# Preparing a second factor in steps of two pieces, with a third staging buffer, and a last sum taken straight from PSUM

## The chip, the cores and the metric

The kernel runs on one core of a Trainium2 chip. The time is device microseconds (us) from start to end of one execution; the kernel before takes 779.91 us, the median of three runs (779.88 to 781.03). A profile is one execution taken by the hardware profiler; its span is 776.9 us. Five engines work side by side: TensorE (PE in the profile; PEld is its weight load), VectorE (DVE), ScalarE (ACT), GpSimd (POOL) and SyncE (SP), whose queue issues most of the transfers. [...]

## What is computed

The first half is an attention without softmax, for 8 batches, 8 heads, 576 tokens and a head size of 64; the second is a feed-forward block with a product of two projections in its middle.

```python
kv = np.einsum('bhsd,bhse->bhde', k, v)
out = np.einsum('bhsd,bhde->bhse', q, kv)
rms = np.sqrt(np.mean(out * out, axis=-1, keepdims=True) + 1e-06)
x = (out / rms * g_norm)          # heads side by side: 4608 tokens x 512
a = x @ w1                        # 512 x 1024
b = x @ w2                        # 512 x 1024
h = a * b @ w3                    # 1024 x 1024
return h @ w_out                  # 1024 x 512
```

All of it is in fp32. Nothing stands between the last two products, so the kernel multiplies `w3 @ w_out` once (1024 x 512, kept in `w3o_sb`) and projects `a * b` with that.

## The kernel before

**Groups.** The tokens are worked in nine groups of 512 (512 of each batch's 576, and one group, number 8, of the 64 that are left of every batch). They run in the order 0 to 6, 8, 7. Each group has two stages. The *gates* (`gates`, called for p = 0 to 3) compute `a * b`: matrix products at L617, ScalarE copies out of PSUM (L630, L752), VectorE sums and products (L753 to L757). The *projection* multiplies `a * b` with the second factor `w3o`. In group 0 that is `project`; from group 1 on it is `project_twice`.

**Fewer products by sums.** Both stages use Winograd's form of Strassen's scheme: a 2 x 2 block product with seven block products instead of eight, paid for by sums of blocks on VectorE. `project_twice` applies it twice: seven outer products, each split again into seven inner ones. For that, each of the seven blocks of the second factor (b11, t1, t2, b22, b12, b21, t4, as `b_blocks` lists them) needs its own four inner combinations t1, t2, t3, t4. They are the same for all groups, so they are computed once.

**Preparing the second factor.** `prepare_b` is a generator that does this while group 1's gates run. Its piece n (0 to 6) takes block n, y: four VectorE subtractions (L810 to L813) put t1, t2 and t4 in a staging buffer of 128 x 768 values and t3 in place over b12 of y; then two transfers on the sync queue store y (L814) and the stage (L817) as part n of the DRAM tensor `w3o_l2`. The stage is `o_sbs[n % 2]`, so piece n may write it only when piece n - 2's store has read it. `o_sbs` holds a group's output too; group 0's output is stored from there (L776). The last block, t4, is also stored as it is, before piece 6 changes it (L799, part 7): the last group multiplies its last product in one level only and needs it unchanged. L812 of piece 6, which writes over a part of it, waits for that store.

**Who calls it.** The loop over groups hands `gates` a function `between`, called twice in each of the four gates of a group, so eight times. Each call first runs one step of the next batch's attention (`steps`): loads of k, v and q (L95, L105, L110), the products of k and v (L326) and with q (L409), the normalisation (L377 to L387, which writes `xn`) and the transposes of q and of `xn`. A transpose goes by way of GpSimd, which splits the words into halves (L284, L286), a DMA transpose on the sync queue (L288), and GpSimd again, which puts them together (L298). `xn` has one buffer and serves as the target of its own transposes, so the next normalisation's last instruction (L387) waits for the L298 of the one before. In group 1, `between` then draws up to three pieces:

```python
for _ in range(2):
    next(preparing, None)
if len(loaded_b) == 0 and next(preparing, 0) == 0:
    for _ in range(3):
        load_b()
```

That makes 3, 3 and 1 pieces in the first three calls; the third also issues the first three `load_b` (L831). These bring parts 0, 1 and 2 back from DRAM into `streams`, three buffers laid over the places of `w3o_sb` and of the blocks t2 and t4. Later parts are loaded one at a time within `project_twice`.

**The order of the work.** TensorE, GpSimd and SyncE run in the order in which the code is written. For VectorE and ScalarE the framework's planner sets the order, but from the last gate of a group to the end of its projection VectorE too follows the code.

**The last group's end.** In `project_twice`, `keep` copies a product's seven blocks from PSUM to SBUF on ScalarE (L900, L901), `add` sums PSUM onto a kept one on VectorE (L928, L929), and `finish` turns seven blocks into four of output by four VectorE sums (L910 to L913) and stores them. The tile `u` that takes u2, u3 and u4 has one buffer. The fifth product is kept as `u3`; its sum with the kept `p5` (L975) is finished as block (1, 1), and u3 itself as block (1, 0). In the last group `last_block` finishes u3, multiplies the last product in one level (L941), adds it (L947) and stores it in two halves (L922).

Of the kernel before, what the change touches and what calls it, by code (L numbers as in the profile page):

```python
# [21 lines left out]
def kernel(  # L22
# [32 lines left out]
    nc = tc.nc  # L55
    PSUM = bass.MemoryType.PSUM
    P = 128
# [9 lines left out]
    N = G // 2  # L67
# [14 lines left out]
    def bank(pool, tag):  # L82
        return pool.tile([P, 512], FP32, name=tag, tag=tag)
# [523 lines left out]
    def late_tile(name):  # L607
        return late_pool.tile([P, 7, P], FP32, name=name[0] if name[0] == "u" else name)

    def winograd(lhsT, rhs, chunks, done, between=lambda: None):  # L610
# [27 lines left out]
        product("s2", "t2", r1)  # L638
        u2 = keep("u2", r1)
        between()  # L640
        product("s4", "b22", r2)
        done("c12", r2, u2)
# [40 lines left out]
    o_sbs, ab_sums, w3o_sums, streams, inner_sums = [], [], [], [], []  # L683
# [103 lines left out]
    def b_blocks():  # L787
        b = {
            (i, j): w3o_sb[:, i * NF:(i + 1) * NF, j * N:(j + 1) * N]
            for i in range(2) for j in range(2)  # L790
        }
        t1, t2, t4 = w3o_sums
        return [b[0, 0], t1, t2, b[1, 1], b[0, 1], b[1, 0], t4]

    def prepare_b():

        for n, y in enumerate(b_blocks()):
            if n == 6:
                nc.sync.dma_start(  # L799
                    out=w3o_l2[7, :, 0:1024].rearrange("p (f n) -> p f n", n=N), in_=y  # L800
                )
            b11, b12, b21, b22 = (
                y[:, 2 * i:2 * i + 2, j * P:(j + 1) * P] for i in range(2) for j in range(2)
            )

            stage = o_sbs[n % 2].rearrange("p m n -> p (m n)")[:, 0:6 * P]
            t1, t2, t4 = (t.rearrange("p (c n) -> p c n", n=P) for t in (
                stage[:, i * 2 * P:(i + 1) * 2 * P] for i in range(3)
            ))
            nc.vector.tensor_sub(t1, b12, b11)  # L810
            nc.vector.tensor_sub(t2, b22, t1)
            nc.vector.tensor_sub(b12, b22, b12)  # L812
            nc.vector.tensor_sub(t4, b21, t2)  # L813
            nc.sync.dma_start(  # L814
                out=w3o_l2[n, :, 0:1024].rearrange("p (f n) -> p f n", n=N), in_=y
            )
            nc.sync.dma_start(out=w3o_l2[n, :, 1024:PART], in_=stage)  # L817
            yield

    loaded_b = []  # L820
# [33 lines left out]
    def project_twice(T, last, ahead):  # L854
        def store(half):
            if T < B:
                rows = out[T * S:T * S + G, :].rearrange("(p j) f -> p j f", j=J)
                nc.sync.dma_start(out=rows[:, 2 * half:2 * half + 2, :], in_=o_sbs[half])
                return
            for m in range(2):  # L860
                for l in range(2):
                    b = 2 * (2 * half + m) + l
                    nc.sync.dma_start(
                        out=out[b * S + G:(b + 1) * S, :], in_=o_sbs[half][l * L:(l + 1) * L, m, :]
                    )

        def products(n, ps=None):

            new = ps is None or n == 5
            if ps is None:  # L870
                ps = [bank(ps_mm, "mm").rearrange("p (i n) -> p i n", n=P) for _ in range(2)]
            a11, a12, a22, s1, s2, s4, s3 = inner[n]
            w = loaded_b[7 * done[T] + n]
            b = w[:, 0:1024].rearrange("p (f n) -> p f n", n=N)
            b11, t3, b21, b22 = (
                b[:, 2 * i:2 * i + 2, j * P:(j + 1) * P] for i in range(2) for j in range(2)
            )
            t1, t2, t4 = (
                w[:, 1024 + 256 * i:1280 + 256 * i].rearrange("p (c n) -> p c n", n=P)
                for i in range(3)  # L880
            )
            seen = set()
            for place, x, y in (
                (0, a11, b11), (3, a12, b21), (1, a22, t4), (2, s1, t1), (6, s2, t2), (5, s4, b22),
                (4, s3, t3),
            ):
                to, i = ps[place // 4], place % 4
                for c in range(2):
                    nc.tensor.matmul(  # L889
                        to[:, i, :], lhsT=x[:, c, :], rhs=y[:, c, :],  # L890
                        start=new and place // 4 not in seen,
                        stop=(c == 1),
                        skip_group_check=True,
                    )
                    seen.add(place // 4)
            return ps

        def keep(name, ps):
            t = late_tile(name)
            nc.scalar.copy(t[:, 0:4], ps[0])  # L900
            nc.scalar.copy(t[:, 4:7], ps[1][:, 0:3])  # L901
            return t

        def finish(z, half, j):

            def wide(i):
                return z[:, i:i + 1].to_broadcast([P, 2, P])

            dst = o_sbs[half][:, :, j * N:(j + 1) * N].rearrange("p m (i n) -> p m i n", n=P)
            nc.vector.tensor_add(z[:, 6], z[:, 6], z[:, 0])  # L910
            nc.vector.tensor_add(z[:, 4:6], z[:, 4:6], wide(6))
            nc.vector.tensor_add(dst[:, 1], z[:, 1:3], wide(4))
            nc.vector.tensor_add(dst[:, 0], z[:, 3:6:2], z[:, 0:3:2])  # L913
            if not last:
                if j == 0:
                    store(half)
            elif (half, j) != (1, 0):
                store_block(half, j)

        def store_block(half, j, a=0, b=2, queue=nc.sync):  # L920
            rows = out[T * S:T * S + G, j * N:(j + 1) * N].rearrange("(p j) f -> p j f", j=J)
            queue.dma_start(  # L922
                out=rows[:, 2 * half + a:2 * half + b, :],
                in_=o_sbs[half][:, a:b, j * N:(j + 1) * N],
            )

        def add(z, ps):
            nc.vector.tensor_add(z[:, 0:4], ps[0], z[:, 0:4])  # L928
            nc.vector.tensor_add(z[:, 4:7], ps[1][:, 0:3], z[:, 4:7])  # L929

        done[T] = len(done)

        def last_block(z):

            a22, t4 = ab[1][:, :, 1], loaded_b[7 * done[T] + 6]
            t4 = t4.rearrange("p (f n) -> p f n", n=N)
            finish(z, 1, 0)
            ps = bank(ps_mm, "mm").rearrange("p (m n) -> p m n", m=2)
            for m in range(2):
                for p in range(NF):  # L940
                    nc.tensor.matmul(  # L941
                        ps[:, m, :], lhsT=a22[:, p, m * P:(m + 1) * P], rhs=t4[:, p, :],
                        start=(m == 0 and p == 0), stop=(p == NF - 1), skip_group_check=True,
                    )
            for m in range(2):
                dst = o_sbs[1][:, m, 0:N]
                nc.vector.tensor_add(dst, dst, ps[:, m, :])  # L947
                store_block(1, 0, m, m + 1, nc.scalar if m else nc.sync)


        r1 = products(0)
        p1 = keep("p1", r1)
        load_b()
        sum_inner(2)
        for f in ahead:
            f()
        r2 = products(1)
        p5 = keep("p5", r2)
        load_b()
        sum_inner(3)  # L960
        products(2, r1)
        z = keep("u2", r1)
        load_b()
        sum_inner(4)
        products(3, r2)
        load_b()
        add(z, r2)
        sum_inner(5)
        finish(z, 0, 1)
        products(4, r1)  # L970
        z = keep("u3", r1)
        load_b()
        if not last:
            sum_inner(6)
        nc.vector.tensor_add(p5, p5, z)  # L975
        finish(p5, 1, 1)
        products(5, r2)
        load_b()
        add(p1, r2)
        finish(p1, 0, 0)  # L980
        if last:
            last_block(z)
        else:
            products(6, r1)
            load_b()
            finish(keep("u4", r1), 1, 0)
# [3 lines left out]
    w3o_l2 = dram.tile([8, P, PART], FP32, name="w3o_l2")  # L990
# [9 lines left out]
    with tc.manual_schedule(  # L1000
# [6 lines left out]
        for e in range(2):  # L1007
            nc.scalar.dma_start(
                out=g_row[:, e * D:(e + 1) * D], in_=g_norm.rearrange("(o d) -> o d", o=1)
# [76 lines left out]
    for n, T in enumerate(groups):  # L1086
        pieces = steps(T + 1) if n + 2 < NG else iter([])

        def between():
            next(pieces, lambda: None)()  # L1090
            if T == 1:
                for _ in range(2):
                    next(preparing, None)
                if len(loaded_b) == 0 and next(preparing, 0) == 0:
                    for _ in range(3):
                        load_b()

        for p in range(NF):
# [28 lines left out]
        last = n + 1 == NG  # L1127
# [6 lines left out]
        preparing = prepare_b()  # L1134
# [32 lines left out]
```

## Time and profile before

| what | value |
|---|---|
| time, median of 3 | 779.91 us |
| span of the profile | 776.9 us |
| TensorE busy | 761.9 us (98%) |
| VectorE busy | 542.0 us (70%) |
| ScalarE busy | 249.5 us (32%) |
| GpSimd busy | 135.1 us (17%) |
| bytes moved by DMA | 132.55 MB |
| group 1, gates (167.84 to 228.49 us) | 60.65 us |
| group 1, projection (228.49 to 251.96 us) | 23.47 us |
| group 3, gates (328.20 to 381.78 us) | 53.58 us |
| group 3, projection (381.78 to 403.66 us) | 21.88 us |

The profile is read by its stretches. The chain of waits, followed back from the last instruction, names for each moment the instruction that the end depended on. The timeline lists each engine's instructions with start, length, engine, line, operation, output and inputs, and in brackets how long the engine had been idle just before and what ended that. The busy times by stretch compare stages of different groups. In the names, `raw` is the memory of the conversion tiles, in which the blocks, the sums and `o_sbs` lie later on; `w3o_l` is the DRAM tensor of the prepared factor.

### The profile page before, as it was taken

The page shows a single profiled execution, that of the slowest core. Times are in us where ns is not written, and L with a number is a line of the kernel's source. Part 1 is how long each engine was busy: PE and PEld are TensorE (multiplying, and loading weights), DVE is VectorE, ACT ScalarE, POOL GpSimd, SP SyncE. Part 2 cuts the span into 40 slices and gives each one's busy share as a digit, 9 for nine tenths or more (in the row PEclk, how much of TensorE's full clock was granted, in tenths as well). Part 3 has the DMA queues.
Part 4 walks back from the last instruction along what each step waited for, and adds up shares of the span by engine and source line. Part 5 has one row for each costly group of instructions (what it writes and reads, how often), then busy time and mean ns, then how long its engine had stood idle before and what let it go on. Part 6 is the DMA issues. An engine that isn't in the chain of part 4 may idle for free.

```text
span 776.9 us, 14423 instructions
## 1 busy us (share of the span) xinstructions
PE 761.9 (98%) x5775; PEld 660.9 (85%) x5775; DVE 542.0 (70%) x1086; ACT 249.5 (32%) x483; POOL 135.1 (17%) x132
## 2 busy tenths in 40 slices
PE   8999999999979999999999999999999999999997
PEld 6455788888869889988998899889988998898896
DVE  6978999439579567945784778567756864594566
ACT  6687643212212332232222322332133222122120
POOL 0000000221330253033204520331144000000000
PEclk9999999999999999999999999999999999999999
DMA  9996650238998844884388448734852470074014
GB/s 316 339 331 182 200 149 30 82 102 260 243 290 281 223 99 109 282 231 110 90 281 220 109 117 271 220 95 133 271 108 51 138 249 0 1 244 143 1 57 167
DMA packets 132775, 132.55 MB, mean 171 GB/s; under 512 B 76644, under 2 KB 120676, under 8 KB 132708
## 3 DMA queue, kind: packets, MB, share of 16 engines
q1 hardware_dynamic: 130256, 116.81, 51.1%
q10 hardware_dynamic: 2452, 14.81, 5.5%
q8 instruction: 46, 0.75, 0.4%
q14 instruction: 21, 0.17, 0.1%
HBM read 100.27 MB, written 16.38 MB: 150 GB/s over the span
## 4 chain that ended last, share of the span: by engine, by line
PE 89%; DVE 5%; DMA 3%; SPq 1%; ACT 1%; issue 1%; POOL 0%; DVEq 0%; ACTq 0%; POOLq 0%
PE mm L617 55%; PE mm L889 21%; PE mm L596 7%; PE at L326 2%; PE at L409 2%; DMA raw<-in_moe_w_out_dram 1%; PE at L583 1%; SPq L288 1%; DVE c L756 1%; DMA w3o_l<-raw 1%; DMA xn<-xT 1%; PE at L345 1%; DVE ab L757 0%; DMA raw<-in_moe_w_dram 0%; DMA out_dram<-raw 0%
## 5 line engine op out<-in xcount | busy, mean ns | idle before, releaser
L617 PE MATMUL mm<-xT,w_sb 128*128 128x256 f32 x768 | 176.2, 379 | 0.0
L617 PEld LDWEIGHTS mm<-xT,w_sb 128*128 128x128 f32 x768 | 145.5, 190 | 20.0 <-issue 0.5
L617 PE MATMUL mm<-xc,ws 128*128 128x256 f32 x576 | 132.2, 382 | 4.9 <-ACT p L630 4.9
L617 PEld LDWEIGHTS mm<-xc,ws 128*128 128x128 f32 x576 | 110.2, 192 | 20.8 <-ACT p L630 5.7
L756 DVE TENSOR_TENSOR c<-mm,u 128x512 f32<-128x512 f32 x36 | 24.9, 691 | 105.8 <-PE mm L617 105.8
L630 ACT COPY u<-mm 128x512 f32<-128x512 f32 x74 | 43.4, 587 | 141.6 <-PE mm L617 133.3
L630 ACT COPY p<-mm 128x512 f32<-128x512 f32 x74 | 43.3, 587 | 87.9 <-PE mm L617 78.5
L617 PE MATMUL mm<-xc,w_sb 128*128 128x256 f32 x288 | 69.3, 383 | 0.0
L889 PE MATMUL mm<-w3o_sb,raw 128*128 128x128 f32 x500 | 62.3, 275 | 0.6 <-DVE raw L849 0.6
L596 PE MATMUL mm<-chunks,ab 128*128 128x512 f32 x128 | 60.2, 601 | 1.7 <-DVE chunks L165 1.6
L617 PE MATMUL mm<-xT,ws 128*128 128x256 f32 x256 | 61.3, 382 | 0.0
L284 POOL COPY xT<-xn 128x1024 uint16<-128x1024 uint16 x26 | 32.3, 1271 | 162.2 <-DVE xn L387 162.1
L617 PEld LDWEIGHTS mm<-xc,w_sb 128*128 128x128 f32 x288 | 53.6, 190 | 7.8 <-ACT u L630 0.3
L757 DVE TENSOR_TENSOR ab<-c 128x256 f32<-128x256 f32 x108 | 58.0, 537 | 3.0
L889 PEld LDWEIGHTS mm<-w3o_sb,raw 128*128 128x128 f32 x500 | 59.0, 192 | 0.9 <-DVE raw L849 0.8
L617 PEld LDWEIGHTS mm<-xT,ws 128*128 128x128 f32 x256 | 48.3, 191 | 6.8
L378 DVE TENSOR_REDUCE inv<-sq 128x8 f32<-128x512 f32 (+1 forms) x40 | 23.4, 626 | 36.0 <-ACT sq L377 36.0
L756 DVE TENSOR_TENSOR c<-p,u 128x512 f32<-128x512 f32 x36 | 25.6, 711 | 27.6 <-ACT u L630 27.4
L889 PE MATMUL mm<-w3o_sb,ab 128*128 128x128 f32 x336 | 43.8, 275 | 0.3 <-DVE ab L851 0.3
L889 PEld LDWEIGHTS mm<-w3o_sb,ab 128*128 128x128 f32 x336 | 41.0, 192 | 0.8 <-DVE ab L851 0.5
L596 PEld LDWEIGHTS mm<-chunks,ab 128*128 128x128 f32 x128 | 21.9, 190 | 22.7 <-issue 15.8
L900 ACT COPY u<-mm 128x512 f32<-128x512 f32 x23 | 13.5, 587 | 85.4 <-DVE raw L913 64.7
(157 smaller groups left out, 1138.7 us busy)
## 6 DMA issues: line engine op xcount, KB each, us to landing
w3o_sb<-w3o_l SPq DMA_DIRECT2D x26, 896.0 KB, 5.0
raw<-in_moe_w_dram SPq DMA_DIRECT2D x31, 512.0 KB, 7.3
raw<-w3o_l SPq DMA_DIRECT2D x13, 896.0 KB, 5.1
w3o_sb<-w3o_l ACTq DMA_DIRECT2D x11, 896.0 KB, 4.7
k_sb<-in_k_dram SPq DMA_DIRECT2D x32, 256.0 KB, 3.7
v_sb<-in_v_dram SPq DMA_DIRECT2D x32, 256.0 KB, 4.3
q_sb<-in_q_dram SPq DMA_DIRECT2D x32, 256.0 KB, 4.2
out_dram<-raw SPq DMA_DIRECT2D x14, 512.0 KB, 3.5
```

The source lines that it names most:

```text
L284: nc.gpsimd.tensor_copy(to, src.rearrange("p a n w -> p w a n"))
L288: nc.sync.dma_start_transpose(out=turned.bitcast(U16).rearrange("p (a t) -> p a t", t=P), in_=apart.bitcast(U16))
L326: nc.tensor.matmul(kv_ps[e * D:(e + 1) * D, r - rs[0], :], lhsT=k_sb[:, e, cols] if j < J else kl[:, 2 * r + e, :], rhs=v_sb[:, e, cols] i ...
L378: nc.vector.tensor_reduce(out=inv[:, i], in_=sq.rearrange("p (h d) -> p h d", d=D), axis=AX.X, op=ALU.add)
L409: nc.tensor.matmul(o_ps[l][tokens, n * D:(n + 1) * D], lhsT=qT[r][rows, e, i, tokens], rhs=kv_b[rows, e, r, :], start=True, stop=True,)
L596: nc.tensor.matmul(sums_ps[half][m], lhsT=w3T[half, c][:, m, :], rhs=chunks[:, c, 1, :], start=(c == 0), stop=(c == KF - 1),)
L617: nc.tensor.matmul(ps[:, u, :], lhsT=lhsT(a_name, u, c), rhs=rhs(b_name, c),  start=(u == 0 and c == 0 and to is None), stop=(c == chunks ...
L630: nc.scalar.copy(t, ps)
L756: nc.vector.tensor_add(c, one, two)
L757: nc.vector.tensor_mul(dst, c[:, 0, :], c[:, 1, :])
L889: nc.tensor.matmul(to[:, i, :], lhsT=x[:, c, :], rhs=y[:, c, :], start=new and place // 4 not in seen, stop=(c == 1), skip_group_check=True,)
L900: nc.scalar.copy(t[:, 0:4], ps[0])
```

## The change

It has two parts. The first spreads the preparation of the second factor: `between` draws two pieces in each of the first three calls and the last piece in the fourth, and a `load_b` is issued for each draw that finds nothing left, so one in the fourth call and two in the fifth. The unchanged last block is stored ahead of all pieces. The stages go round three buffers: piece 4 takes the place of block t1 (`w3o_sums[0]`), which piece 1 has stored by then, and the other six take the two of `o_sbs` in turn (0, 1, 0, 1, -, 0, 1). This is to even out what the preparation asks of VectorE and the queues, and to take away the wait of the last piece for a store that was issued just before.

The second part changes the last group alone. The sum of the fifth product with `p5` is taken straight from PSUM, and u3 is copied besides, for block (1, 0); that block is finished ahead of the sum of the sixth product. This is to let the sum start without the copy.

```diff
 def prepare_b():
+    nc.sync.dma_start(
+        out=w3o_l2[7, :, 0:1024].rearrange("p (f n) -> p f n", n=N), in_=b_blocks()[6]
+    )
     for n, y in enumerate(b_blocks()):
-        if n == 6:
-            nc.sync.dma_start(
-                out=w3o_l2[7, :, 0:1024].rearrange("p (f n) -> p f n", n=N), in_=y
-            )
         ...
-        stage = o_sbs[n % 2].rearrange("p m n -> p (m n)")[:, 0:6 * P]
+        stage = w3o_sums[0].rearrange("p f n -> p (f n)") if n == 4 else (
+            o_sbs[(n - n // 5) % 2].rearrange("p m n -> p (m n)")
+        )
+        stage = stage[:, 0:6 * P]
...
-        def last_block(z):
+        def last_block():
             ...
-            finish(z, 1, 0)
...
         products(4, r1)
+        if last:
+            add(p5, r1)
         z = keep("u3", r1)
         load_b()
         if not last:
             sum_inner(6)
-        nc.vector.tensor_add(p5, p5, z)
+            nc.vector.tensor_add(p5, p5, z)
         finish(p5, 1, 1)
+        if last:
+            finish(z, 1, 0)
         products(5, r2)
         load_b()
         add(p1, r2)
         finish(p1, 0, 0)
         if last:
-            last_block(z)
+            last_block()
...
             if T == 1:
                 for _ in range(2):
-                    next(preparing, None)
-                if len(loaded_b) == 0 and next(preparing, 0) == 0:
-                    for _ in range(3):
+                    if next(preparing, 0) == 0 and len(loaded_b) < 3:
                         load_b()
```

## The prediction

> **What bounds the kernel now.** I read the page first. TensorE is busy almost throughout, so only idle time of TensorE, or time after its last matmul, can be won.
>
> ```profile
> PE 761.9 (98%) x5775; PEld 660.9 (85%) x5775; DVE 542.0 (70%) x1086; ACT 249.5 (32%) x483; POOL 135.1 (17%) x132
> ```
>
> Then the chain of waits: it is nothing but matmuls from 252 to 762 us; it leaves TensorE between 164 and 232 us (group 1, where the changed `prepare_b` runs) and after 762 us (the last group's end). So I took the busy times by stretch for the gates and the projection of group 1, and of group 3, which has the same matmuls and attention steps and no second factor to prepare. Columns: stretch, its length, then busy time (and instructions) of PE, PEld, DVE, ACT, POOL, the granted clock, DMA share, GB/s.
>
> ```profile
> 167.84:228.49 60.65, 55.77 (x433) 47.95 (x432) 40.70 (x78) 15.65 (x34) 18.29 (x17) 0.97 0.93 270
> 228.49:251.96 23.47, 22.60 (x198) 22.11 (x196) 22.36 (x50) 5.12 (x10) 2.44 (x2) 1.00 0.73 241
> ...
> 328.20:381.78 53.58, 53.58 (x435) 46.96 (x433) 29.43 (x58) 15.75 (x34) 18.71 (x17) 1.00 0.54 149
> 381.78:403.66 21.88, 21.88 (x197) 21.88 (x196) 20.74 (x51) 5.12 (x10) 0.00 (x0) 1.00 0.69 239
> ```
>
> Group 1 loses 60.65 - 53.58 = 7.07 us in its gates and 23.47 - 21.88 = 1.59 us in its projection: 8.66 us is the most that the first edit can bring. The timeline of TensorE there shows where:
>
> ```profile
> 186.72 1.99 PE L617 MATMUL mm<-xc,ws 128*128 128x256 f32 x8 [0.57 <-ACT p L630]
> ...
> 218.07 3.50 PE L617 MATMUL mm<-xc,ws 128*128 128x256 f32 x8 [4.31 <-ACT p L630]
> 221.37 2.11 PE L617 MATMUL mm<-xT,ws 128*128 128x256 f32 x8
> 223.31 3.62 PE L617 MATMUL mm<-xT,w_sb 128*128 128x256 f32 x16
> ...
> 231.64 0.71 PE L889 MATMUL mm<-w3o_sb,raw 128*128 128x128 f32 x4 [0.58 <-DVE raw L849]
> 232.65 0.71 PE L889 MATMUL mm<-w3o_sb,ab 128*128 128x128 f32 x4 [0.30 <-DVE ab L851]
> ```
>
> Idle 0.57 + 4.31 us, and the 16 matmuls after the long gap take 223.31 - 218.07 = 5.24 us, where two eights elsewhere take 3.46 (193.73 to 195.46 is 1.73 each): 1.78 more. That is 6.66 of the 7.07; in the projection 0.88 of 1.59 is idle. Who held ScalarE's copy `p`? VectorE's timeline:
>
> ```profile
> 205.93 0.38 DVE L757 TENSOR_TENSOR ab<-c 128x256 f32<-128x256 f32 x1
> 212.02 0.42 DVE L812 TENSOR_TENSOR raw<-raw 128x256 f32<-128x256 f32 x1 [5.70 <-DMA w3o_l<-raw]
> 213.49 1.29 DVE L387 TENSOR_TENSOR xn<-at,inv 128x512 f32<-128x512 f32 x2 [1.04 <-POOL xT L298]
> ```
>
> L812 rewrites the last block in place and waits for the store of it (L799), issued only at 208.91. Behind it, L387 needs `xn` back from GpSimd's L298, which ran from 210.97 to 213.46. So there are two waits, 1.5 us apart in their ends: removing the first alone brings at most 1.5 us.
>
> The tail: `u` has one buffer, so the copy of `u3` waits for VectorE's last read of `u2`, and the sum L975 waits for the copy.
>
> ```profile
> 764.86 0.42 DVE L913 TENSOR_TENSOR raw<-u 128x256 f32<-128x256 f32 x1
> 765.37 0.59 ACT L900 COPY u<-mm 128x512 f32<-128x512 f32 x1 [6.41 <-DVE raw L913]
> 765.85 0.48 ACT L901 COPY u<-mm 128x384 f32<-128x384 f32 x1
> 766.37 1.09 DVE L975 TENSOR_TENSOR p<-p,u 128x896 f32<-128x896 f32 x1 [1.09 <-ACT u L901]
> ```
>
> [...] after 4.31 us idle, eight matmuls took 3.30 us for 1.73; after 0.57 us, nearly none of it. [...] L848 takes 1.27 us beside GpSimd's copy at 228.87, and 0.43 us in group 3. [...] the changed order does make the copy wait for VectorE. No run yet shows its cost.
>
> **The change part by part.** *The last block sent first.* The store moves ahead of piece 0, to about 177.1 us: 0.57 us of issue and 512 KB more before the other stores. L812's 5.70 us wait goes.
>
> *Two pieces a step.* Piece 2 no longer stands before the k and v loads and the q transposes on the sync queue. Before, that queue stood until piece 2 was computed (its store issued at 184.35), and the transposes went at 189.60. Now: last block 177.1, pieces 0 and 1 until about 180.9, loads of k and v (as before, 4.3 us) until about 185, transposes at 185. But data counts too: 0.5 MB + 2 x 0.9 MB of stores + 1.25 MB of loads = 3.55 MB, at the 390 GB/s that the filled slices there show 9.1 us, from 178 to about 187.5. I take the transposes as 3 to 3.5 us earlier than before, not the 4.6 that the queue alone would give. Then all behind moves: GpSimd's q copies from 196.38 to 193, its split of `xn` (L284) from 198.77 to 195.4, the transposes of `xn` from 204.65 to about 198 (they have no piece 4 or 5 before them either, since these come after). Landing and start of L298 6.3 us later as before (204.65 to 210.97): 204.3 to 206.8.
>
> VectorE reaches L387 at about 206.3. From its start to TensorE's restart the trace needs 218.07 - 213.49 = 4.58 us; TensorE runs dry at 213.76, or 213.1 with the 0.67 us won before. So L387 may start as late as 208.5; at 206.8 there is 1.7 us to spare, and the 4.31 + 1.78 us go.
>
> *The early gap.* On VectorE piece 2 now stands behind the two sums L378 (184.58 before); four instructions of 0.35 us ahead of them go, ScalarE's square root and the copy `p` (186.10) come 1.4 us earlier, TensorE wanted it at 186.15: 0.57 + 0.1 us go.
>
> *The third buffer.* Piece 4 writes in t1's place, which piece 1's store has left by about 186. Pieces 5 and 6 wait for the stores of pieces 2 and 3, issued at about 189 to 191 and down 4.8 us later (194.49 to 199.27 is that row's figure): 194 to 196, and VectorE gets there after 196.65. So no wait, where before L810 stood 1.48 us.
>
> *The loads of pieces* start at about 206, not 213, behind piece 4's store; they take 7.3 to 8.4 us, and the projection needs the first at 220. Cost nothing.
>
> *The projection.* Its losses come from GpSimd's L298 at 228.87, which lies on VectorE's L848 and L849. With L387 7 us earlier the second pair of transposes goes when the first piece has landed (about 213 to 214), and L298 runs at about 217 to 221; the inner sums begin at about 221. I take 1.2 us of 1.59, bounds 0 and 1.6.
>
> So group 1: 6.5 us of 7.07 in the gates (the rest has no row that names it), and 1.2.
>
> *The last group.* The sum needs no copy: it starts at about 765.3, not 766.37, and costs 1.18 us (768.96 to 770.14 on the rows L928 and L929, the same shapes from PSUM) for 1.12. VectorE's end comes 1.0 us earlier. `finish(z, 1, 0)` moves ahead of `add(p1, r2)`: the same four instructions, no waits, since the copy (now 766.0 to 767.0) is done before 768.1. But the 256 KB store of block (0, 0) is now issued 0.5 us before the last 256 KB and not 2 us: 512 KB at the 340 GB/s of the last slices take 1.5 us from about 773.1, so they end at 774.7, not 775.4. Gain 0.7 us, bounds 0.4 and 1.0.
>
> Sum: 6.5 + 1.2 + 0.7 = 8.4; 779.9 - 8.4 = 771.5 us.
>
> **The rivals.** *Half of it, 775.9 us.* The transposes are held by the filled DMA engines (0.93 busy in this stretch), `xn` comes back at 211, TensorE idles 2.5 us with half the slow restart (0.9), the projection stays: 7.07 - 2.5 - 0.9 - 0.4 + 0.7 = 4.0 us. For it: only 1.7 us to spare in a chain of estimates. Against it: the transposes stand behind less data than before in every step.
>
> *No difference, 779.2 us.* `xn` comes back as late as before, and only the tail is won. For it: L298 ended 1.5 us after L812's wait and would replace it. Against: it needs all the 3 us on the sync queue to be lost.
>
> *Slower, 784.9 us.* The loads of pieces stand in the sync queue until their buffers' stores are down, with k and v loads and transposes behind them; if the first piece landed only at 232, TensorE would idle 11 us at 221 and restart slowly (1.8): 779.9 - 7.07 - 0.7 + 11 + 1.8. For it: three such waits in a row are new. Against: they can start 7 us earlier than now.
>
> **How the numbers follow.** The forecast, with its unknown terms between their bounds (770.0 to 773.5), 0.75; half 0.14; none 0.06; slower 0.05. Low end: 8.66 + 1.0 us won and some spread, 769.8. High end 775.6, which takes in a part of the half case. Faster by over 0.2% (under 778.3): 0.75 + 0.14 = 0.89; within 0.2%: 0.06; slower: 0.05.
>
> **What would show it.** Right: no gap over 1 us on TensorE between 168 and 230 us; no VectorE wait for a store of the second factor at L815 (L812 before); L298 of `xn` ending before 208.5 us; group 1's gates at about 54 us and its projection under 23; in the last group VectorE's sum starting within 0.1 us of the end of L916 (L913 before), and the last store issued 7.8 us after that end and not 8.75 (765.28 to 774.03). Wrong: VectorE's L387 waiting for GpSimd beyond 208.5, the q transposes issued after 187, or TensorE waiting for a piece's load in the first projection.

## The result, and the profile after

The changed kernel takes 770.9 us (770.41 to 772.34, four runs) against 780.47 us for the kernel before, measured beside it: a ratio of 0.988, with a 95% interval of 0.9862 to 0.9897. The prediction had said 771.5. Of the runs below, two of the four of `prepare_alone` and one of the kernel before beside it took 1757 to 3722 us, far outside all others, and the ratios leave them out.

The busy times by stretch, for the gates and the projection of group 1 in the changed kernel (same columns as before):

```profile
168.84:222.40 53.56, 53.56 (x434) 46.94 (x433) 41.94 (x78) 15.86 (x34) 18.42 (x17) 1.00 1.01 296
222.40:245.10 22.70, 22.12 (x198) 21.96 (x197) 21.60 (x49) 5.13 (x10) 2.44 (x2) 1.00 0.94 272
```

The gates take 53.56 us, not 60.65, as group 3 does (53.58), and TensorE is busy for all of it. The projection takes 22.70 us, not 23.47. From the end of VectorE's last read of `u2` to the end of the span the last group takes 769.2 - 758.42 = 10.78 us, before 776.9 - 765.28 = 11.62. The sum is 7.09 + 0.77 + 0.84 = 8.70 us, within the 8.0 to 10.8 us that the interval of the times allows. The medians differ by 9.57 us; the profiled execution of the kernel before took 778.64 us, less than its median, and where the other 0.87 us lie was not found. The two spans differ by 7.7 us, because group 1 started 1.0 us later in this execution (168.84 against 167.84): in the runs below that start lies anywhere between 166.8 and 169.7 us, in a part of the program that no edit touches. So stretches of group 1 are compared from its start, and the tail from the end of the last read of `u2`.

VectorE's timeline in the changed kernel, at the place where it stood for 5.70 and 1.04 us before (the line numbers of `prepare_b` are 3 higher, those of `project_twice` too):

```profile
201.80 0.42 DVE L815 TENSOR_TENSOR raw<-raw 128x256 f32<-128x256 f32 x1
202.13 0.42 DVE L816 TENSOR_TENSOR raw<-raw 128x256 f32<-128x256 f32 x1
204.06 1.28 DVE L378 TENSOR_REDUCE inv<-sq 128x8 f32<-128x512 f32 x2 [1.50 <-ACT sq L377]
205.33 0.69 DVE L756 TENSOR_TENSOR c<-mm,u 128x512 f32<-128x512 f32 x1
...
206.10 1.11 DVE L757 TENSOR_TENSOR ab<-c 128x256 f32<-128x256 f32 x1
207.14 1.28 DVE L387 TENSOR_TENSOR xn<-at,inv 128x512 f32<-128x512 f32 x2
```

Columns of a timeline: start, length, engine, line, and in brackets the idle time before and what ended it. Neither the in-place subtraction (L815) nor the normalisation (L387) waits. GpSimd had returned `xn` just before, at 206.93, and ScalarE's copies `p`, at 212.24 and 213.96, wait only for their matmuls (1.35 and 1.14 us), where before they waited 6.71 us for the sum L756 (217.43). GpSimd's return of `xn` before, then its instructions after:

```profile
210.97 2.48 POOL L298 COPY xT<-xn 128x1024 uint16<-128x1024 uint16 x2 [9.99 <-DMA xn<-xT]
```

```profile
193.84 2.60 POOL L298 COPY qT<-q_sb 128x1024 uint16<-128x1024 uint16 x2 [9.91 <-DMA q_sb<-qT]
196.39 2.41 POOL L284 COPY xT<-xn 128x1024 uint16<-128x1024 uint16 x2
204.69 2.24 POOL L298 COPY xT<-xn 128x1024 uint16<-128x1024 uint16 x2 [5.89 <-DMA xn<-xT]
```

The last group's end: the sum (L931, L932) starts with no gap after L916, and ScalarE's copy follows it (759.05; L931 ends at 759.01).

```profile
758.00 0.42 DVE L916 TENSOR_TENSOR raw<-u 128x256 f32<-128x256 f32 x1
758.33 0.68 DVE L931 TENSOR_TENSOR p<-mm,p 128x512 f32<-128x512 f32 x1
...
758.93 0.55 DVE L932 TENSOR_TENSOR p<-mm,p 128x384 f32<-128x384 f32 x1
...
759.05 0.59 ACT L903 COPY u<-mm 128x512 f32<-128x512 f32 x1 [6.96 <-DVE p L931]
```

### The profile page after: what moved, and what is told of

Its sections match the earlier page's. It is cut to its first block, busy times and chain, and to the rows that moved or that the text cites. A ratio compares the mean times of both kernels' runs of the same rounds, so it can differ in the third digit from the quotient of the medians.

```text
span 769.2 us, 14423 instructions
## 1 busy us (share of the span) xinstructions
PE 759.5 (99%) x5775; PEld 659.6 (86%) x5775; DVE 542.2 (70%) x1087; ACT 250.1 (33%) x483; POOL 134.9 (18%) x132
## 4 chain that ended last, share of the span: by engine, by line
PE 93%; DMA 4%; DVE 1%; ACT 1%; SPq 1%; issue 0%; DVEq 0%; ACTq 0%
PE mm L617 59%; PE mm L892 22%; PE mm L596 6%; PE at L326 3%; PE at L409 2%; DMA raw<-in_moe_w_dram 2%; DMA raw<-in_moe_w_out_dram 1%; PE at L583 1%; DMA v_sb<-in_v_dram 1%; PE at L345 0%; SPq L95 0%; PE at L427 0%; DMA out_dram<-raw 0%; PE at L442 0%; SPq L190 0%
## 5 line engine op out<-in xcount | busy, mean ns | idle before, releaser
L617 PE MATMUL mm<-xc,ws 128*128 128x256 f32 x576 | 130.5, 379 | 0.1
L756 DVE TENSOR_TENSOR c<-mm,u 128x512 f32<-128x512 f32 x36 | 24.9, 690 | 106.0 <-PE mm L617 106.0
L630 ACT COPY u<-mm 128x512 f32<-128x512 f32 x74 | 43.4, 587 | 137.5 <-PE mm L617 132.5
L630 ACT COPY p<-mm 128x512 f32<-128x512 f32 x74 | 43.4, 586 | 85.4 <-PE mm L617 82.4
L378 DVE TENSOR_REDUCE inv<-sq 128x8 f32<-128x512 f32 (+1 forms) x40 | 23.4, 626 | 36.5 <-ACT sq L377 36.5
L756 DVE TENSOR_TENSOR c<-p,u 128x512 f32<-128x512 f32 x36 | 26.5, 737 | 28.1 <-ACT u L630 27.9
```

The source lines that it names most:

```text
L378: nc.vector.tensor_reduce(out=inv[:, i], in_=sq.rearrange("p (h d) -> p h d", d=D), axis=AX.X, op=ALU.add)
L617: nc.tensor.matmul(ps[:, u, :], lhsT=lhsT(a_name, u, c), rhs=rhs(b_name, c),  start=(u == 0 and c == 0 and to is None), stop=(c == chunks ...
L630: nc.scalar.copy(t, ps)
L756: nc.vector.tensor_add(c, one, two)
```

## Experiments

Two theories stood against each other for the first part. The prediction's: two waits stand one behind the other on VectorE, for the store of the last block and for GpSimd's return of `xn`; sending the block early takes the first, and the pace of two pieces a step takes the second by bringing the transposes forward. The rival: the store's place is all, and pace and third buffer only cost instructions on the way. This table has what every run showed; gates and projection are group 1's, from the first matmul of one stretch to the first of the next; "end" is from the last read of `u2` to the end of the span. All three are of one profiled execution each. `prepare_alone` and `prepare_again` are the same kernel: the stretches are of the second, the ratio of the two executions of the first that count.

| kernel | gates | projection | end | ratio of times to before (95%) |
|---|---|---|---|---|
| before | 60.65 | 23.47 | 11.62 | 1 |
| changed | 53.56 | 22.69 | 10.78 | 0.988 (0.9862 to 0.9897) |
| prepare_alone, prepare_again | 53.56 | 23.38 | 11.52 | 0.989 (0.9862 to 0.9918) |
| tail_alone | 60.30 | 23.70 | 10.78 | 0.9984 (0.9972 to 0.9997) |
| early_block | 53.56 | 23.04 | 11.55 | 0.9907 (0.9888 to 0.9927) |
| late_block | 55.04 | 23.23 | 11.60 | 0.991 (0.9895 to 0.9925) |
| two_stages | 57.14 | 22.48 | 11.53 | 0.9965 (0.9952 to 0.9977) |
| three_a_step | 53.92 | 24.87 | 11.58 | 0.9923 (0.9899 to 0.9946) |
| early_fixed | 61.75 | 23.45 | 11.59 | 0.9994 (0.9984 to 1.0004) |
| after_fixed | 53.55 | 22.69 | 10.79 | 0.988 (0.9861 to 0.9899) |
| old_finish_order | 53.55 | 22.49 | 10.48 | 0.9882 (0.9858 to 0.9906) |
| loads_later | 53.55 | 25.14 | 10.80 | 0.9922 (0.9901 to 0.9943) |
| early_and_tail | 53.56 | 25.07 | 10.41 | 0.9906 (0.9886 to 0.9926) |

**The two parts, one at a time.** `prepare_alone` is the changed kernel with the last group as it was before; `tail_alone` is the kernel before with the change's edits to `project_twice` and nothing else.

> The change without its last-group part: early last block, two pieces a step, third buffer. If the two parts are independent, group 1's gates take 53.6 us and its projection 22.7 us as in the changed kernel (7.9 us less than before), the end from the last read of u2 is 11.6 us as before, and the time is 780.2 - 7.9 = 772.3 us. If the tail had a part in the gain beyond its 0.8 us, it stays above 773.

> The change without its last-group part, once more for its stretches: gates of group 1 53.6 us, projection 22.7, end 11.6 us after the last read of u2.

> The last-group part alone. From the end of VectorE's last read of u2 to the end of the span 11.62 us become 10.8 us; group 1 stays at 60.7 and 23.5 us. Time 779.4 us, too close to 780.2 for the times; the trace's stretch decides. Rival: the end is set by the stores, and nothing is gained (11.6 us).

The parts are independent, as far as these stretches can tell. The preparation alone gives the same 53.56 us in the gates, and an end of 11.52 us as before (11.62). It took 770.11 and 772.19 us in `prepare_alone` and 770.42 us in `prepare_again`, where 772.3 was expected. Its projection takes 23.38 us, not the 22.7 expected, with TensorE waiting 0.66 us there for the load of a piece. The tail alone gives the same 10.78 us at the end, to the hundredth, and its time lies within 0.03 to 0.28% under that of before. So the stores do not set the end alone, and the tail is worth 0.8 us.

**The early store alone.** In the kernel before:

```diff
 def prepare_b():
+    nc.sync.dma_start(out=w3o_l2[7, ...], in_=b_blocks()[6])
     for n, y in enumerate(b_blocks()):
-        if n == 6:
-            nc.sync.dma_start(out=w3o_l2[7, ...], in_=y)
```

> The kernel before with one edit: the unchanged last block is stored ahead of the pieces; still three pieces a step and two stages. The prediction's theory: GpSimd's return of xn takes the place of the wait for the store, 1.5 us earlier at most, so group 1's gates still lose 5 us or more and the time is 778.5 us or more. Rival: the wait for the store was the cause; or the planner, which no longer sees that wait, puts the normalisation (L387) behind the sum that frees p1, so that its wait holds nobody: then the 4.31 us gap and the slow restart go, the gap of 0.6 us near 186 us stays, and the time is about 774 us.

A surprise for the theory: the gates take 53.56 us, all 7.09 us are won, and the gap near 186 us, which even the rival let stand, is gone too. The profile shows how the long gap went. The return of `xn` is as late as ever and L387 does wait for it, but it stands behind the sum that frees `p1` (the third L756), no longer ahead of it. VectorE's timeline in this kernel:

```profile
208.58 0.69 DVE L756 TENSOR_TENSOR c<-p,u 128x512 f32<-128x512 f32 x1 [0.71 <-ACT u L630]
...
210.11 0.68 DVE L756 TENSOR_TENSOR c<-mm,p 128x512 f32<-128x512 f32 x1
214.93 1.29 DVE L387 TENSOR_TENSOR xn<-at,inv 128x512 f32<-128x512 f32 x2 [4.14 <-POOL xT L298]
```

The planner, which sets VectorE's order here, had changed it with the edit. Nothing on the path stands behind the 4.14 us of waiting, so they cost nothing. Whether the early store or the new order brought the gain, this run can't say. Hence the next two.

**The order held.** The same kernel, and the changed one as a control, with VectorE's order in the third gate of group 1 written out: the normalisation's last part behind the first sum and ahead of the other two, where it stands both before and after the change.

```diff
-        fs[second].append((a.finish, 1))
+        if b == 2:                       # group 1: first two steps of the normalisation here
+            def half():
+                held.append(a.product(1))
+                next(held[0])
+                next(held[0])
+            fs[second].append((half,))
+        else:
+            fs[second].append((a.finish, 1))
...
             multiply(name, one, two)
+            if held and name == "c12":   # its last step here
+                all_of(held.pop())
             ready(name)
...
+            if T == 1 and p == 2:
+                with tc.manual_schedule(engines={mybir.EngineType.DVE}):
+                    gates(T, p, between)
+                    run(sum_ab(p))
+                continue
```

> The kernel before with the last block sent first, and VectorE's order in the third gate of group 1 written out so that the normalisation (L387) stands behind the first of the three sums and ahead of the other two, where it stands in the kernel before and in the changed one. The prediction's theory of two waits in a row: L387 waits for GpSimd's return of xn until about 213 us after a group start of 168, the sum that frees p1 follows it, and TensorE idles about 3 to 4.5 us and restarts slowly: gates of group 1 58 to 60.5 us, time about 778. Rival: the wait for the store was all, and the planner's order is incidental: gates 53.6 to 54.5 us.

> The control: the changed kernel with the same written-out order in the third gate of group 1. With two pieces a step xn comes back before L387 is reached, so nothing waits: gates 53.6 us, time as the changed kernel, 770.9. If writing the order out itself costs something, it shows here.

With the order held, the early store alone is worth nothing: 0.9994, with an interval that holds 1. VectorE and TensorE in that kernel (L767 and L639 are L756 and L630 of before):

```profile
206.26 0.24 DVE L384 RECIPROCAL inv<-inv 128x16 f32<-128x16 f32 x1
212.95 1.29 DVE L387 TENSOR_TENSOR xn<-at,inv 128x512 f32<-128x512 f32 x2 [6.45 <-POOL xT L298]
...
216.12 0.69 DVE L767 TENSOR_TENSOR c<-mm,p 128x512 f32<-128x512 f32 x1
```

```profile
217.54 3.78 PE L626 MATMUL mm<-xc,ws 128*128 128x256 f32 x8 [4.97 <-ACT p L639]
221.11 3.11 PE L626 MATMUL mm<-xT,ws 128*128 128x256 f32 x8
```

The wait for GpSimd takes the place of both waits of before: 6.45 us on VectorE, 4.97 us on TensorE, and the first eight matmuls after it take 3.57 us (217.54 to 221.11) instead of 1.73. The gates take 61.75 us, more than the 60.5 expected and than before: the next eight matmuls are slow too (2.95 us, 221.11 to 224.06, where the kernel before took 1.94). The control, with the same order, two pieces a step and the third buffer, has gates of 53.55 us and takes 770.93 us. So in this order the early store is not enough, as the prediction said, and pace and third buffer bring the rest; and there is a second way to the same gain, an order in which the late return holds nobody. That order without the early store was not tried.

**Pace and third buffer without the early store.** The changed preparation with the block's store back in front of piece 6; the last group as before.

```diff
-        nc.sync.dma_start(out=w3o_l2[7, ...], in_=b_blocks()[6])
         for n, y in enumerate(b_blocks()):
+            if n == 6:
+                nc.sync.dma_start(out=w3o_l2[7, ...], in_=y)
```

> The changed preparation (two a step, third buffer), but the last block's store back in front of piece 6. The in-place subtraction of piece 6 then waits for a store issued behind pieces 4 and 5 in the sync queue, at about 207 us, down at 212 us. In the program's order on VectorE that subtraction stands between the two halves of the normalisation, ahead of the sum that frees p1: so TensorE waits again, gates of group 1 about 58 us or more (4 us or more lost of the 7). Rival: pace and buffers were what mattered, and the store's place costs under 1 us (gates under 54.6 us).

The gates take 55.04 us: 1.48 us are lost, less than the 4 expected. VectorE (here L816 is the in-place subtraction):

```profile
205.81 0.68 DVE L387 TENSOR_TENSOR xn<-at,inv 128x512 f32<-128x512 f32 x1
209.40 0.42 DVE L816 TENSOR_TENSOR raw<-raw 128x256 f32<-128x256 f32 x1 [2.90 <-DMA w3o_l<-raw]
209.74 0.68 DVE L387 TENSOR_TENSOR xn<-at,inv 128x512 f32<-128x512 f32 x1
```

The wait is there, in the middle of the normalisation, but only 2.90 us long, and TensorE idles 0.38 us for it, and 0.57 us earlier as in the kernel before. So pace and third buffer bring 5.6 of the 7.09 us by themselves (with the order that the planner gives them here, in which the in-place subtraction stands between the two halves), and the early store the rest.

**The third buffer.** The changed preparation with piece n in stage n mod 2; the last group as before.

```diff
-            stage = w3o_sums[0].rearrange("p f n -> p (f n)") if n == 4 else (
-                o_sbs[(n - n // 5) % 2].rearrange("p m n -> p (m n)")
-            )
-            stage = stage[:, 0:6 * P]
+            stage = o_sbs[n % 2].rearrange("p m n -> p (m n)")[:, 0:6 * P]
```

> The changed preparation with the two stages of before (piece n in stage n mod 2), no third buffer; last-group part as before. Theory: piece 4 then waits on VectorE for piece 2's store, issued at about 193 us and down at about 198, with nothing urgent behind it before 200; piece 6 waits for piece 4's store, issued behind the transposes at about 203 us and down at 208, and it stands on VectorE between the two sums of the normalisation, ahead of the sum that frees p1: xn and p1 come some 2 us later, and TensorE loses 0 to 3 us in group 1's gates (53.6 to 56.6 us). Rival: the third buffer is needed for nothing, gates 53.6 us.

The gates take 57.14 us, 3.58 more than with the third buffer and more than the 56.6 expected at most. It is the wait that was expected: piece 6 stands between the two sums of the normalisation and waits for piece 4's store, and the second sum, behind it in VectorE's order, starts only at 207.29. VectorE, then TensorE (L810 is piece 6's first subtraction):

```profile
202.42 0.69 DVE L378 TENSOR_REDUCE inv<-sq 128x8 f32<-128x512 f32 x1 [1.02 <-ACT sq L377]
206.95 0.43 DVE L810 TENSOR_TENSOR raw<-raw 128x256 f32<-128x256 f32 x1 [3.84 <-DMA w3o_l<-raw]
207.29 0.68 DVE L378 TENSOR_REDUCE inv<-sq 128x8 f32<-128x512 f32 x1
```

```profile
210.43 1.99 PE L617 MATMUL mm<-xc,w_sb 128*128 128x256 f32 x8 [3.31 <-ACT u L630]
```

**Three a step.** Early block and third buffer, three pieces a step and the three loads together, as before; the last group as before.

```diff
                 for _ in range(2):
-                    if next(preparing, 0) == 0 and len(loaded_b) < 3:
+                    next(preparing, None)
+                if len(loaded_b) == 0 and next(preparing, 0) == 0:
+                    for _ in range(3):
                         load_b()
```

> Early last block and third buffer, but three pieces a step and the three loads together, as before. If the pace of two is needed to get the transposes ahead of piece 2, GpSimd's L298 on xn starts at 211 us as before, the gap of 0.6 us near 186 us stays, and the gates lose over 3 us. If the planner's order (normalisation behind the sum that frees p1) is what counts, only the 0.6 us stay: gates about 54.3 us, time about 773 us.

GpSimd's L298 on `xn` starts at 211.02 us, as late as before, and the planner again has L387 behind the third sum, where its wait of 3.93 us holds nobody: gates 53.92 us, and no gap near 186 us, which was expected to stay. The projection loses 24.87 - 22.69 = 2.2 us; TensorE waits there 0.81 and 1.25 us for loads of pieces. That this comes from the three loads being issued together was not tried by itself, and the projection varies without any edit to it: `early_block` and `early_and_tail` have the same group 1 and take 23.04 and 25.07 us.

This run and `two_stages` also part the pace from the third buffer in what they do to GpSimd's return of `xn`. From the start of group 1 it begins at 43.1 us with three pieces a step, third buffer or not (before, `three_a_step`), and at 35.9 to 36.0 with two, third buffer or not (changed, `two_stages`). So it is the pace that brings the transposes forward.

**The finish order.** The changed kernel with block (1, 0) finished last, as before.

```diff
         finish(p5, 1, 1)
-        if last:
-            finish(z, 1, 0)
         products(5, r2)
         ...
         if last:
+            finish(z, 1, 0)
             last_block()
```

> The changed kernel, but block (1,0) finished where it was before, after block (0,0). VectorE has the same work, so the last store is issued as soon; block (0,0)'s 256 KB go 1.5 us earlier and no longer overlap the last two stores. The end after the last read of u2 is 10.4 us instead of 10.8 if those stores' overlap costs 0.4 us. Rival: VectorE then waits for the sixth product's last matmul (its first sum would come at 760.98 where the matmuls end at about 760.95), and the end is 10.8 us or later.

The end takes 10.48 us instead of 10.78. VectorE doesn't wait for the sixth product (L931 follows L916 at 760.38 without a gap), and the last stores land 1.9 us after their issue, against 2.3 to 2.4 in the changed kernel. So moving `finish(z, 1, 0)` cost 0.3 us; the other kernels with that move end in 10.78 to 10.80 us, the other one without it (`early_and_tail`) in 10.41. This has the lowest median of the study, 770.23 us; 0.3 us is too little for the times to tell it from the changed one.

**The loads later.** The changed kernel with the second and third load one step later, behind the second transposes of `xn`.

```diff
-                    if next(preparing, 0) == 0 and len(loaded_b) < 3:
+                    if next(preparing, 0) == 0 and len(loaded_b) < (1 if calls[0] < 6 else 3):
                         load_b()
```

> The changed kernel, but the second and third loads of pieces are issued one step later, behind the second transposes of xn. Those then no longer stand behind a ring of loads: GpSimd's L298 on xn at 226.35 comes about 5 us earlier. The wait of 0.6 us in the first projection (TensorE held at 231.95 us) goes if it was piece 3's load, slowed by transposes and loads beside it: projection 21.9 us instead of 22.7, time about 770.1. Rival: the second or third piece comes too late for its product, and TensorE waits 1 to 5 us at 225 or 229 us: time 772 to 776.

The time is that of the rival, 773.67 us, projection 25.14, but its mechanism is a part only: TensorE waits 1.09 us for a load, at 227.51. The transposes still kept the sync queue until 222.08, so the two loads went then; and GpSimd's L298 moved from 226.35 to 221.25, exactly onto the first inner sums. VectorE and TensorE in this kernel:

```profile
221.64 1.26 DVE L851 TENSOR_TENSOR raw<-ab 128x256 f32<-128x256 f32 x1
222.93 1.26 DVE L852 TENSOR_TENSOR raw<-raw,ab 128x256 f32<-128x256 f32 x1
224.22 0.43 DVE L853 TENSOR_TENSOR raw<-ab,raw 128x256 f32<-128x256 f32 x1
```

```profile
224.24 1.17 PE L893 MATMUL mm<-w3o_sb,raw 128*128 128x128 f32 x8 [0.58 <-DVE raw L852]
225.71 0.71 PE L893 MATMUL mm<-w3o_sb,ab 128*128 128x128 f32 x4 [0.29 <-DVE ab L855]
227.51 1.58 PE L893 MATMUL mm<-w3o_sb,raw 128*128 128x128 f32 x12 [1.09 <-DMA w3o_sb<-w3o_l]
```

Beside GpSimd's copy a sum of 0.43 us takes 1.26, and TensorE has the same two gaps (0.58 and 0.29 us) as in the kernel before.

**The least edit.** The kernel before with the early store only, the planner's own order, and the sum from PSUM with block (1, 0) finished last.

> The kernel before with only the last block sent first (three pieces a step, two stages, the planner's own order) and, in the last group, the sum from PSUM with block (1,0) finished last. If pace and third buffer add only what the projection of group 1 shows (23.0 against 22.7 us), it takes 53.6 us in the gates, 23.0 in the projection, 10.5 us at the end, and 771 us in time.

Gates 53.56 us and end 10.41 us as expected, but the projection takes 25.07 us, not 23.0: TensorE waits 1.90 us for a piece's load. The time is 772.87 us, ratio 0.9906. It doesn't beat the changed kernel; but the two intervals overlap, and so do those of `early_block` and `prepare_alone`. What pace and third buffer add to the early store, once the planner has its own order, these times don't resolve.

## Why the prediction was right

The forecast was 8.4 us; 8.70 us show in the stretches. The terms were less exact than the sum: the gates gave 7.09 us where 6.5 was said, the projection 0.77 where 1.2 was said, the tail 0.84 where 0.7 was said. Two of the prediction's own signs of being wrong came true without harm: the q transposes went at 188.19, which is 187.2 with the later start of the group taken off, after 187; and TensorE waited 0.58 us for what is most likely a piece's load.

**The two waits in a row** were the right reading: the early store alone, in the same order, is worth nothing (`early_fixed`). The sentence that removing the first wait alone brings at most 1.5 us was true only of that order. The prediction treated VectorE's order as given, though the planner sets it in this stage; in `early_block` the planner moved L387, and 7.09 us came. In the changed kernel it stayed ahead of the sums, so the prediction's path is the one that was taken; that the planner left it there was not foreseen, only assumed.

**The transposes forward.** From the start of group 1, the q transposes went 2.4 us earlier (189.60 - 167.84 = 21.8 before, 188.19 - 168.84 = 19.4 after) where 3 to 3.5 were said, but GpSimd's q copies came 3.5 us earlier (28.5 to 25.0) and its return of `xn` 7.3 us earlier (43.1 to 35.9), where 6.7 was said. L387 started 38.3 us after the group's start; the step allowed up to 40.7. So 2.4 us were to spare, where 1.7 was said. The mechanism was right: `two_stages` and `three_a_step` show that the return follows the pace.

**The early gap** went, but not for the reason given, so this term was right by luck. The first L378 came 1.46 us earlier against the group's start (16.74 to 15.28), and with it the copy `p`. VectorE before, then in the changed kernel (L813 is the last instruction of a piece in the first, the first one of a piece in the second):

```profile
184.24 0.42 DVE L813 TENSOR_TENSOR raw<-raw 128x256 f32<-128x256 f32 x1
184.58 1.27 DVE L378 TENSOR_REDUCE inv<-sq 128x8 f32<-128x512 f32 x2
```

```profile
184.12 1.26 DVE L378 TENSOR_REDUCE inv<-sq 128x8 f32<-128x512 f32 x2
185.31 0.41 DVE L813 TENSOR_TENSOR raw<-raw 128x256 f32<-128x256 f32 x1
```

But the pace did not do it. `late_block` has two pieces a step, its L378 comes at 16.74 as before, and TensorE has the same gap; `early_block` has three, and its L378 comes at 15.28, with the piece behind its first part. TensorE in `late_block`, then VectorE in `early_block` (where L809 to L812 are a piece):

```profile
186.29 1.99 PE L617 MATMUL mm<-xc,ws 128*128 128x256 f32 x8 [0.57 <-ACT p L630]
```

```profile
184.98 0.67 DVE L378 TENSOR_REDUCE inv<-sq 128x8 f32<-128x512 f32 x1
185.66 0.42 DVE L809 TENSOR_TENSOR raw<-raw 128x256 f32<-128x256 f32 x1
186.00 0.68 DVE L378 TENSOR_REDUCE inv<-sq 128x8 f32<-128x512 f32 x1
186.59 0.42 DVE L810 TENSOR_TENSOR raw<-raw 128x256 f32<-128x256 f32 x1
```

In every trace of the table the gap is there without the early store and gone with it. The early store changes where the planner puts the piece; why, no run shows.

**The restart.** The 1.78 us were counted as part of the long gap and went with it; the granted clock in the gates rose from 0.97 to 1.00. The slow matmuls stood behind 4.31 us of idle time (the first eight took 3.30 us, eights elsewhere 1.73), and the gap is gone. In `early_fixed`, behind 4.97 us, the first eight took 3.57 us, and the granted clock was 0.94 (167.80 to 228.00); in `two_stages`, behind 3.31 us, they took 1.83. The half restart that a rival put behind 2.5 us of idle time was an estimate and is not shown by these runs.

**The third buffer** was right in that pieces 5 and 6 wait for nothing in the changed kernel. `two_stages` shows that without it the new pace loses 3.58 us.

**The projection** was the step that was wrong in its working. It said that the second transposes of `xn` would go at 213 to 214 and GpSimd's L298 run at 217 to 221. They went when they should, but held the sync queue far longer:

```profile
213.16 0.43 SPq L834 DMA_DIRECT2D raw<-w3o_l  x1
213.71 9.96 SPq L288 DMA_TRANSPOSE xn<-xT  x2
```

The L298 started at 226.35. It fell on a later inner sum (L850 at 227.70, 1.37 us) that TensorE did not yet need; the first three took 0.42 to 0.43 us. That is why the gaps of before went nevertheless, by luck: in `loads_later`, some 4 us earlier against the group's start, the same copy brings them back. What was won is 0.77 us, where 1.2 was said, and even that is one execution: three other kernels with the changed group 1 (`prepare_again`, `after_fixed`, `old_finish_order`) took 22.49 to 23.38 us there, the two with that of before 23.47 and 23.70. In the changed kernel's trace TensorE stands 0.58 us, from 231.93. The trace names ScalarE's copy of `u2`, which ends at 232.45, but by the program the product that starts there doesn't need it. It reads piece 3, whose load was issued at 225.94 and took 6.4 us, to about 232.3; so the load is the likelier cause. In `late_block`, `prepare_again`, `three_a_step` and `early_and_tail` the traces put waits of TensorE in this projection down to such loads (0.62, 0.66, 0.81 and 1.90 us). That the loads are slow (6.4 us for this one, where the median of such loads on ScalarE's queue is 4.6 in the changed kernel) because the transposes run beside them is argued, not shown: `loads_later`, meant to part them, ran into another collision.

**The tail** was right. Its two terms were both larger: VectorE's end came 1.31 us earlier (from the last read of `u2` to the last store's issue 8.75 us before, 7.44 after) where 1.0 was said, since the sum overlaps the end of L916 and L949 no longer stands 0.1 us for anything; and the crowded stores gave back 0.47 us (issue to end of span 2.87 before, 3.34 after) where 0.3 was allowed. `old_finish_order` shows most of the cause of the second: with block (0, 0) stored earlier, 0.30 us of it go.

**The rivals.** "Half of it" and "no difference" needed the return of `xn` to stay late; that happens in `early_fixed`, not here. "Slower" needed late loads; at most 0.6 us was lost to one.

## What to carry to other kernels

When two waits stand in a row on an engine, the end of the second is the bound on what removing the first can bring, as long as the order of instructions stays. Where a planner sets that order, an edit to a dependence can change it far from its place: look at the new order before pricing a wait, and hold the order fixed in an experiment that is to price the edit itself. What a wait costs is what stands behind it in its engine's queue: 4.14 us of waiting cost nothing behind the sum that frees a buffer (`early_block`, gates 53.56 us), and 6.45 us ahead of it cost 8 us of TensorE (`early_fixed`, gates 61.75 us).

## What the runs showed of the hardware that was not expected

The 17 executions of `two_stages` lie between 774.3 and 779.3 us, the 20 of the kernel before beside them between 778.0 and 781.8, and the four of the changed kernel within 2 us. In `two_stages` the time goes with the granted clock: the five lowest times have a clock of 0.997 to 1.000, the five highest one of 0.994 to 0.997. TensorE's gap is 3.31 us long in the profiled execution, whose clock is 1.000, and the eight matmuls behind it take 1.83 us, as they do behind 0.57 us in the kernel before (186.72 to 188.55), so no slow restart shows there. Behind 4.31 and 4.97 us (the kernel before and `early_fixed`) eight took 3.30 and 3.57 us. That the gap of 3.31 us brings the slow restart in some executions and not in others is a guess; these clocks fit it, but no trace of `two_stages` with a low clock was taken.

The sync queue took 5.22 and 4.70 us over two DMA transposes of the same size that took 2.58 us together in group 3 (352.17, before the change). The DMA engines were busy for 0.94 to 1.01 of the stretch here, for 0.54 there. Whether the queue stood for the DMA engines or for earlier transfers was not tried.
